# A retention and feed-forward kernel on one core: q scaled after the products instead of before, a new order of work, and other placements

## The chip, the cores and the metric

The kernel runs on one core of a Trainium2 chip. Its engines work at the same time, each through its own list of instructions in order: TensorE (PE; the loads of its weights are PEld), VectorE (DVE), ScalarE (ACT), GpSimd (POOL) and SyncE (SP). Here GpSimd and SyncE only issue DMA transfers. The metric is the device time of one execution in microseconds (us), as the median of several.

## The reference

Eight batches of eight heads, 576 positions of 64 values: each head's scores are multiplied by a matrix that falls off with distance and is zero for later positions, without a softmax. The result, 4608 rows of 512, goes through two layers of 2048 and 512 with a leaky ReLU between. All inputs are float32.

```python
scores = scale * np.matmul(q, k.transpose(0, 1, 3, 2))
gamma = 1.0 - 2.0 ** (-5.0 - np.arange(H, dtype=np.float32))
rel = pos[:, None] - pos[None, :]
Dmat = np.where(rel >= 0, gamma[:, None, None] ** rel[None, :, :], 0.0)
attn_out = np.matmul(scores * Dmat[None], v)
x = attn_out.transpose(0, 2, 1, 3).reshape(B * S, H * D)
h = x @ w_in
out = np.maximum(0.01 * h, h) @ w_out
```

## The kernel before

**Tiling.** The 4608 rows are cut into 36 blocks u of 128 rows (two chunks of 64) and nine groups g of 512 rows (four blocks). All heads of a block are handled together.

**Attention of a block.** Three loads (`ld{u}.0`, `.1`, `.2` for q, k, v; line 346) bring float32 tiles `t`. The falling-off factor gamma^(i-j) is split: q is multiplied by gamma^r times the scale, v by gamma^-r, where r is the place of the row in a stretch of 256 rows. `cq`, `ck`, `cv` (lines 371, 375, 381) make 16-bit tiles from them: k is cast, q and v are scaled by a table in the constants `cs`. On VectorE a scaling is one instruction; on ScalarE it is eight, one for each head. q and k are then turned, by TensorE (`tp`, line 411, copied out of PSUM by `yt`, line 418) for the first eight blocks and by a DMA transpose (`tr`, line 397) for the others. `sa` (line 445) makes the scores, `mk` (line 460) masks them, `sb` (line 454) makes the products of k and v, `st` (lines 485 to 491) adds them to a running state, `sx` (lines 503 and 506) casts the state. `ow` and `ca`, or `oa` in the first four blocks (line 542), add the products of scores and v and of q and state in the PSUM tile `ot`. `x` (line 591) copies that out as `xT`, the input of the first layer. `ot` has two halves, and block u+2 uses the half of block u again.

**The two layers.** The first layer of groups 0 and 1 is plain (`h`, line 640, and the leaky ReLU `l`, line 647). From group 2 on (`a{g}.{n}`, line 833) and in the second layer (`b{g}`, line 911), seven products of sums of quarters take the place of eight. The sums are made on VectorE, of the weights once (lines 686 and 715) and of the data for each group (lines 813 and 887). Partial results are copied out of PSUM by `cA`, `u2` and `k5` (lines 772, 783, 786) and added on VectorE (lines 857 and 947).

**What sets the order.** Nothing is scheduled while the kernel is built. `ORDER` is one long list of job names written out by hand or by another program, and each engine gets its jobs in the sequence of that list. `ENGINE` says which of VectorE and ScalarE does a job where either could. `+n@p` is n products of the constant tile `idle` (line 980), whose results nobody reads. The loads of the first twelve blocks and the weights all go through GpSimd's queue, but for q and k of block 0; later q and k go through SyncE's. The weights come in four quarters each (`wi`, line 612, and `wo`, line 621) and are cast on the way. A block's q, k and v buffers are used again four blocks later (`ld=4`).

Of the kernel before, what the change touches and what calls it, by code (L numbers as in the profile page):

```python
# [33 lines left out]
class Plan:  # L34
# [52 lines left out]
    for eng, names in {  # L87
        "DVE": """
            ck0 cq0 sx0.0 yt0.0 cq1 sx0.1 cv1 cq2 sx1.0 yt2.1 ck3 cq3 yt3.1 cv3 sx2.1 yt3.0 cq4 cv4 x3 ck5 cq5
            cv5 yt5.1 cq6 sx5 cv6 cq7 ck7 cv7 yt7.0 b0.cA cv8 ck10 sx8.0 cv9 cq9 cq11 cq12 cv10 b1.cA cv13 ck15  # L90
            cv14 cq14 cv15 cq15 sx13.1 sx14 cq16 cv16 cv17 cq17 cq18 a2.3.k5 sx17.0 cv18 sx18 cq19 a3.1.u2 x17
            cv20 ck21 cq21 sx19 a3.2.k5 cq22 cv22 sx20 ck23 cv23 cq23 x20 cv24 cq25 sx23 a4.2.cA cv25 a4.2.u2
            cq26 cq27 cv27 sx25 a5.0.u2 a5.0.k5 cq28 cq29 cv29 ck30 cq30 cv30 ck31 cv31 cq32 sx30 cq33 ck33
            a6.0.cA cv33 cv34 ck34 cq35 cq34 a6.2.cA b5.u2 cv35 a6.3.u2 x32 a7.0.cA x33 a7.0.k5 b5.21 a7.1.cA
            b6.11 b6.u2 a7.3.cA a7.3.u2 a8.0.k5 b7.k5 a8.2.u2 a8.2.k5 b7.21 a8.3.u2 b8.21
        """,
        "ACT": """
            cv0 yt0.1 x0 ck1 ck2 yt1.1 yt1.0 cv2 yt2.0 x1 sx1.1 sx2.0 x2 sx3.0 ck4 sx3.1 yt4.1 yt4.0 ck6 sx4.1
            x4 yt5.0 x5 yt6.0 yt6.1 sx6 yt7.1 sx7 x7 x6 ck8 b0.11 cq8 ck9 b0.u2 cq10 b0.k5 cv11 ck12 sx9 x8 ck11
            cv12 sx10 cq13 b0.21 x9 ck13 sx11 b1.11 sx12 x10 b1.u2 x11 ck14 a2.0.cA b1.k5 a2.0.u2 a2.0.k5 x12  # L100
            a2.1.cA a2.1.u2 x13 a2.1.k5 ck16 ck17 sx15 a2.2.cA a2.2.u2 b1.21 a2.2.k5 sx16 x14 a2.3.cA x15
            a2.3.u2 ck18 b2.cA a3.0.cA b2.11 a3.0.u2 a3.0.k5 a3.1.cA cv19 b2.u2 x16 a3.1.k5 ck19 b2.k5 a3.2.cA
            ck20 cq20 a3.2.u2 cv21 b2.21 ck22 x18 a3.3.cA a3.3.u2 a3.3.k5 x19 b3.cA a4.0.cA b3.11 sx21 ck24
            a4.0.u2 a4.0.k5 cq24 a4.1.cA a4.1.u2 sx22.1 a4.1.k5 x21 b3.u2 ck25 b3.k5 ck26 sx24 a4.2.k5 x22 cv26
            a4.3.cA x23 a4.3.u2 a4.3.k5 ck27 b3.21 a5.0.cA b4.cA ck28 cv28 sx26.0 b4.11 x24 ck29 a5.1.cA a5.1.u2
            a5.1.k5 x25 sx27 sx28 b4.u2 a5.2.cA x26 sx29 b4.k5 a5.2.u2 a5.2.k5 x27 a5.3.cA ck32 a5.3.u2 cv32
            a5.3.k5 cq31 b4.21 x28 x29 sx31.1 a6.0.u2 a6.0.k5 sx32 b5.cA a6.1.cA b5.11 a6.1.u2 x30 a6.1.k5 x31
            a6.2.u2 a6.2.k5 sx33 b5.k5 ck35 a6.3.cA a6.3.k5 sx34 sx35.0 a7.0.u2 b6.cA a7.1.u2 a7.1.k5 a7.2.cA
            a7.2.u2 b6.k5 a7.2.k5 x34 x35 a7.3.k5 a8.0.cA b6.21 a8.0.u2 b7.cA b7.11 a8.1.cA b7.u2 a8.1.k5
            a8.1.u2 a8.2.cA a8.3.cA a8.3.k5 b8.cA b8.u2 b8.k5 b8.11x so8.11x b8.11y  # L110
# [941 lines left out]
```

## Time and profile before

| | us |
|---|---|
| median of three runs | 279.86 |
| lowest and highest of the three | 279.4, 282.3 |
| the profiled execution, its time | 279.54 |
| the profiled execution, its span | 277.7 |

The span runs from the first to the last instruction; the time has 1.8 us more around it. The granted clock of TensorE was 0.999 over the span. In the rows further down an engine's busy time is the union of its instructions' spans, and TensorE's ends are modelled: a matmul of 256 columns is shown with 273 ns, while eight of them in a row take 0.87 us. A row of the stages begins with the stretch and its length, and ends with the clock, the share of time in which the DMA engines were busy, and GB/s.

How fast DMA moved things (mean busy share of the 16 DMA engines, in 40 slices) and what each kind of load took from its issue to its landing (us, median):

```profile
DMA  7999999997899999799999998799041100300123
...
t<-in_q_dram POOLq DMA_DIRECT2D x10, 256.0 KB, 8.5
t<-in_k_dram POOLq DMA_DIRECT2D x10, 256.0 KB, 6.5
w_in<-in_moe_w_in_dram POOLq DMA_DIRECT2D x4, 512.0 KB, 7.8
w_out<-in_moe_w_out_dram POOLq DMA_DIRECT2D x4, 512.0 KB, 9.7
```

### The profile page before, as it was taken

What the parts mean: (1) busy time and instruction counts of PE and PEld (TensorE: products, weight loads), DVE (VectorE), ACT (ScalarE), POOL (GpSimd) and SP (SyncE); (2) the same over time, 40 slices, a digit from 0 to 9 for tenths busy, and PEclk for the clock granted to TensorE, in tenths of its full rate; (3) what the DMA queues carried; (4) which work ended last, traced back from release to release, by engine and by line L of the source; (5) the groups of instructions that cost most, each with busy time, mean ns of one, the idle gap of its engine ahead of it and who ended that gap; (6) DMA issues with size and microseconds to landing.
All of it is one profiled execution on the core that took longest, in us unless ns stands there. A gap on an engine that the chain in (4) does not pass through costs nothing.

```text
span 277.7 us, 10117 instructions
## 1 busy us (share of the span) xinstructions
PE 268.1 (97%) x4337; PEld 224.4 (81%) x4337; DVE 229.8 (83%) x431; ACT 206.7 (74%) x459; POOL 72.4 (26%) x92
## 2 busy tenths in 40 slices
PE   6878999999999999999999999999999999999994
PEld 2545688888888888888888888888888888888884
DVE  2767767989998999899999999898989885955761
ACT  3846678769977998999889998899765756665630
POOL 8959696401211313222113321120011000200200
PEclk9999999999999999999999999999999999999999
DMA  7999999997899999799999998799041100300123
GB/s 219 224 240 238 293 287 269 277 216 177 208 256 220 220 295 227 173 236 230 257 222 255 183 228 183 170 247 219 20 139 74 44 2 2 153 0 0 78 97 132
DMA packets 94364, 50.04 MB, mean 180 GB/s; under 512 B 83312, under 2 KB 88560, under 8 KB 94320
## 3 DMA queue, kind: packets, MB, share of 16 engines
q1 hardware_dynamic: 82624, 21.37, 40.4%
q0 software_dynamic: 11264, 27.79, 36.1%
q8 instruction: 34, 0.56, 0.8%
q10 hardware_dynamic: 432, 0.24, 0.3%
q14 instruction: 10, 0.08, 0.1%
HBM read 36.81 MB, written 9.44 MB: 167 GB/s over the span
## 4 chain that ended last, share of the span: by engine, by line
PE 91%; DMA 5%; POOL 1%; ACT 1%; issue 1%; DVE 1%; POOLq 0%
PE acc L911 39%; PE acc L833 32%; PE acc L640 10%; DMA t<-in_k_dram 5%; PE ot L542 5%; PE sc L454 2%; PE sc L445 2%; PE sc L911 1%; POOL t L346 1%; PE acc L411 1%; DVE s L487 0%; POOL w_in L612 0%; ACT st L503 0%; DVE qk L375 0%; DVE s L460 0%
## 5 line engine op out<-in xcount | busy, mean ns | idle before, releaser
L911 PEld LDWEIGHTS <-gt 128*128 128x128 f16 x720 | 69.8, 98 | 8.4
L346 POOL DMA_DIRECT2D t<-in_v_dram x40 | 34.2, 857 | 100.5 <-DVE v L375 64.0
L911 PE MATMUL acc<-w_out,gt 128*128 128x256 f16 x416 | 51.5, 273 | 0.0
L833 PEld LDWEIGHTS <-w_in 128*128 128x128 f16 x448 | 42.4, 98 | 5.6
L853 ACT ACTIVATE gt<-acc 128x512 f16<-128x512 f32 x56 | 33.4, 599 | 16.6 <-PE acc L833 16.4
L861 ACT ACTIVATE gt<-sum 128x512 f16<-128x512 f32 x56 | 34.8, 633 | 4.7 <-DVE sum L857 4.7
L911 PE MATMUL acc<-w_mix,gt 128*128 128x256 f16 x288 | 36.2, 273 | 0.0
L833 PEld LDWEIGHTS <-w_sum 128*128 128x128 f16 x336 | 32.2, 98 | 4.1
L833 PE MATMUL acc<-xs,w_sum 128*128 128x256 f16 x224 | 33.6, 273 | 0.0
L833 PE MATMUL acc<-xT,w_in 128*128 128x256 f16 x224 | 33.5, 273 | 0.0
L833 PE MATMUL acc<-xs,w_in 128*128 128x256 f16 x224 | 33.4, 273 | 0.0
L730 POOL DMA_DIRECT2D out_dram<-osb x16 | 11.5, 718 | 83.9 <-ACT acc L772 38.5
L640 PE MATMUL acc<-xT,w_in 128*128 128x256 f16 (+2 forms) x272 | 30.8, 266 | 0.7 <-ACT qkT L418 0.4
L911 PEld LDWEIGHTS <-mix 128*128 128x128 f16 x288 | 28.1, 98 | 3.3
L460 DVE TENSOR_TENSOR s<-sc,cs 128x512 f16<-128x512 f32 x36 | 24.6, 684 | 4.4 <-PE sc L445 2.3
L640 PEld LDWEIGHTS <-w_in 128*128 128x128 f16 x272 | 22.0, 98 | 5.8 <-issue 0.9
L857 DVE TENSOR_TENSOR sum<-acc,k 128x512 f32<-128x512 f32 x28 | 19.2, 686 | 7.9 <-PE acc L833 5.7
L647 ACT ACTIVATE gt<-acc 128x512 f16<-128x512 f32 x32 | 18.2, 601 | 6.3 <-PE acc L640 6.2
L786 ACT COPY k<-acc 128x512 f32<-128x512 f32 x29 | 17.0, 588 | 7.5 <-PE acc L833 3.7
L375 DVE TENSOR_TENSOR qk<-t,cs 128x512 f16<-128x512 f32 x30 | 20.5, 684 | 2.3 <-DMA t<-in_q_dram 2.3
L591 ACT CAST xT<-ot 128x512 f16<-128x512 f32 x31 | 18.2, 588 | 4.6 <-PE ot L542 4.6
L381 ACT ACTIVATE v<-t,cs 128x64 f16<-128x64 f32 x72 | 18.3, 343 | 4.1 <-DMA t<-in_v_dram 3.4
(69 smaller groups left out, 469.7 us busy)
## 6 DMA issues: line engine op xcount, KB each, us to landing
t<-in_v_dram POOLq DMA_DIRECT2D x32, 256.0 KB, 5.1
out_dram<-osb POOLq DMA_DIRECT2D x16, 512.0 KB, 4.5
t<-in_k_dram SPq DMA_DIRECT2D x22, 256.0 KB, 4.8
t<-in_q_dram SPq DMA_DIRECT2D x22, 256.0 KB, 5.0
t<-in_q_dram POOLq DMA_DIRECT2D x10, 256.0 KB, 8.5
t<-in_k_dram POOLq DMA_DIRECT2D x10, 256.0 KB, 6.5
w_in<-in_moe_w_in_dram POOLq DMA_DIRECT2D x4, 512.0 KB, 7.8
w_out<-in_moe_w_out_dram POOLq DMA_DIRECT2D x4, 512.0 KB, 9.7
```

The costliest lines, as they stand in the source:

```text
L346: engine[eng].dma_start(out=t[CH * j : CH * j + rows], in_=(q, k, v)[x][b, :, CH * w : CH * w + rows, :].rearrange("h t d -> t h d"),)
L375: engine[e].tensor_tensor(out=view[0](out), in0=view[1](t32[u, 2 * x][:]), in1=view[1](decay(u, x)), op=MUL)
L381: nc.scalar.mul(out=out[:, at(h), :], in_=t32[u, 2 * x][:, h, :], mul=tab_sb[:, w, x, h : h + 1])
L460: landed[u] = nc.vector.tensor_tensor(out=s[:], in0=sc[:, :, 0], in1=mask_sb.unsqueeze(1).unsqueeze(1).to_broadcast([P, 2, NP, CH]), op=MUL,)
L591: moved[u] = copies[xe](out=x_of(u).rearrange("q c (j t) -> q j c t", j=2), in_=at)
L640: nc.tensor.matmul(out=a[:, n, :], lhsT=w_in16[:, c, (f0 + n) * P : (f0 + n + 1) * P], rhs=x[:, c, t0 : t0 + nt], start=(n == 0 and c == 0 ...
L647: nc.scalar.activation(out=y[:, f0 : f0 + nf, t0 : t0 + nt], in_=a[:], func=mybir.ActivationFunctionType.Lrelu)
L833: nc.tensor.matmul(out=r[:, f, :], lhsT=w[:, c, (2 * n + f) * P : (2 * n + f + 1) * P], rhs=rhs[:, c, :], start=fresh and c == 0 and f == ...
L853: w = op(what, "ACT", lambda: nc.scalar.activation(out=to(), in_=r[:], func=lr), after, [y], [r])
L857: what, "DVE", lambda: nc.vector.tensor_tensor(out=s[:], in0=r[:], in1=plus[:], op=ADD),
L861: f"l{g}.{n}.{what}", "ACT", lambda: nc.scalar.activation(out=to(), in_=s[:], func=lr), [j], [y],
L911: nc.tensor.matmul(out=(r[tb] if isinstance(r, tuple) else r)[:, tb, :], lhsT=lhs[n]()[:, f, tb * P : (tb + 1) * P], rhs=rhs[n][:, f, :], ...
```

## The change

The factor of q depends on the row alone, and a row of q becomes a column of `ot` for each head. So `cq` is now a plain cast, and `x`, now always on VectorE, multiplies `ot` by a table `q_tab` while it copies it out. The table has a value for each head, place in the stretch of 256 rows, and row. Four VectorE jobs `tb0` to `tb3` make it at the start from two small factors in `cs`, which grows from 148 to 236 values a partition. The tile `stmp` goes (the state is scaled in place), the float states get a pool of three of their own, `idle` becomes a piece of `w_mix`, and a tile `pad` makes the weights begin at a multiple of 512 bytes. `ENGINE` and `ORDER` are new. In `ORDER`, q goes first on SyncE, and GpSimd issues the loads of blocks 0 to 3 ahead of the first quarter of w_in. There are 38 idle products instead of 33. 24 of the 36 `cq` are now on ScalarE (6 before); 24 `ck` are, as before; 6 `cv` (9 before); 19 `sx` jobs (25 before); 94 of the 111 `cA`, `u2` and `k5` (87 before).

```diff
 CFG = dict(
     ap=4,
+    fp=3,
...
-    ld0.1 ld0.2 ld0.0 ld1.0 ld1.1 ld2.1 ck0 ld2.0 cq0 ld1.2 cv0 cq1 ld2.2 +13@3 tp1.0@0 wi1 tp0.0@1 tp0.1@2 sb0 +4@3
+    tb1 tb0 ld0.0 ld0.2 ld0.1 ld1.1 tb3 ld1.2 cq0 ck0 +9@3 tp0.0@3 tb2 ld1.0 yt0.0 +6@1 tp0.1@0 cv0 ld2.1 yt0.1 ck1
...
-    idle = const_pool.tile([P, TOK], F16, name="idle")
-    warm = const_pool.tile([P, 1], FP, name="warm")
+    q_tab = const_pool.tile([P, NB, NP, CH], FP, name="q_tab")
+    pad = const_pool.tile([P, 48], FP, name="pad")
+    warm = pad[:, 0:1]
+    idle = w_mix[:, 2, 0:2].rearrange("p f n -> p (f n)")
...
+    def q_table():
+        for a in range(NB):
+            def run(a=a):
+                nb = CH // FINE
+                nc.vector.tensor_tensor(
+                    out=q_tab[:, a].rearrange("p c (b r) -> p c b r", b=nb),
+                    in0=fine_sb.unsqueeze(2).to_broadcast([P, NP, nb, FINE]),
+                    in1=coarse_sb[:, :, a].unsqueeze(3).to_broadcast([P, NP, nb, FINE]), op=MUL,
+                )
+            steep.append(add(f"tb{a}", "DVE", run))
...
-        def cq():
-            scaled(t[:, 0], 0, qe, lambda h: 2 * (h % NP) + h // NP, (by_half, in_halves))
+        def plain(x, e):
+            copies[e](out=by_half(t[:, x]), in_=in_halves(t32[u, x][:]))
...
-            moved[u] = copies[xe](out=x_of(u).rearrange("q c (j t) -> q j c t", j=2), in_=at)
+            moved[u] = nc.vector.tensor_tensor(
+                out=x_of(u).rearrange("q c (j t) -> q j c t", j=2), in0=at, in1=by_place, op=MUL
+            )
...
-        copied[u] = add(f"x{u}", xe, cp, [j], [xT[u // 4]], [ot_banks])
+        copied[u] = add(f"x{u}", "DVE", cp, [j] + [steep[p] for p in sorted({p0, p1})], [xT[u // 4]], [ot_banks])
```

GpSimd's list at the start, before and after; `t_0`, `t_1`, `t_2` are tiles of q, k and v, and a block whose chunks lie in two batches takes two loads (x2). Before, the loads of blocks 0 (v), 1 and 2, a quarter of w_in, then blocks 3 and 4:

```order
L346 DMA t_2_137<-in_v_dram 128x8x64
L346 DMA t_0_141<-in_q_dram 128x8x64
L346 DMA t_1_143<-in_k_dram 128x8x64
L346 DMA t_1_145<-in_k_dram 128x8x64
L346 DMA t_0_149<-in_q_dram 128x8x64
L346 DMA t_2_152<-in_v_dram 128x8x64
L346 DMA t_2_165<-in_v_dram 128x8x64
L612 DMA w_in_122<-in_moe_w_in_dram 128x4x512
L346 DMA t_1_220<-in_k_dram 128x8x64
L346 DMA t_0_226<-in_q_dram 128x8x64
L346 DMA t_1_260<-in_k_dram 64x8x64 x2
L346 DMA t_2_293<-in_v_dram 128x8x64
```

and after, from the third of these loads on:

```order
L364 DMA t_2_146<-in_v_dram 128x8x64
L364 DMA t_0_167<-in_q_dram 128x8x64
L364 DMA t_1_185<-in_k_dram 128x8x64
L364 DMA t_0_206<-in_q_dram 128x8x64
L364 DMA t_2_221<-in_v_dram 128x8x64
L364 DMA t_2_223<-in_v_dram 128x8x64
L364 DMA t_1_264<-in_k_dram 128x8x64
L364 DMA t_0_314<-in_q_dram 128x8x64
L642 DMA w_in_124<-in_moe_w_in_dram 128x4x512
L364 DMA t_0_326<-in_q_dram 64x8x64 x2
L642 DMA w_in_124<-in_moe_w_in_dram 128x4x512
L364 DMA t_1_361<-in_k_dram 64x8x64 x2
```

The three loads of block 3 (v, k, q) moved from behind the first quarter of w_in to ahead of it, and the three quarters that follow stand between single loads of block 4.

VectorE's list at the start, before; here `t` and `qk` are a block's tiles, `s_` the float states, `st_` the cast ones:

```order
L371 CAST qk_147<-t_1_135 128x2x4x64
L375 TENSOR_TENSOR qk_147<-t_0_139,cs 128x2x4x64
L375 TENSOR_TENSOR qk_163<-t_0_141,cs 128x2x4x64
L485 COPY s_222<-sc 128x256
L418 COPY qkT<-acc 128x512
L375 TENSOR_TENSOR qk_228<-t_0_149,cs 128x2x4x64
L375 TENSOR_TENSOR v_258<-t_2_152,cs 128x512
```

and after:

```order
L382 TENSOR_TENSOR q_tab<-cs 128x256 x4
L407 TENSOR_TENSOR v_183<-t_2_139,cs 128x512
L403 CAST qk_188<-t_1_143 128x2x4x64
L509 COPY s_208<-sc 128x256
L511 TENSOR_TENSOR s_208<-sc,s_208 128x256
L407 TENSOR_TENSOR v_218<-t_2_146,cs 128x512
```

The scalings of q of blocks 0 to 2 have left this list, the table and v of block 0 have come into it.

VectorE's list where blocks 2 and 3 end, after the change (`ot` times the table into `xT`, among states and masks):

```order
L619 TENSOR_TENSOR xT<-ot,q_tab 128x2x4x64
L511 TENSOR_TENSOR s_485<-sc,s_412 128x256
L484 TENSOR_TENSOR s_487<-sc,cs 128x512
L619 TENSOR_TENSOR xT<-ot,q_tab 128x2x4x64
L484 TENSOR_TENSOR s_554<-sc,cs 128x512
L619 TENSOR_TENSOR xT<-ot,q_tab 128x2x4x64 x2
```

Before, the results of blocks 0 to 2 were copies in ScalarE's list, and block 3's alone was here; now all four are multiplications here, the last two behind the mask of block 3.

More of the change, by code (lines that the diff above doesn't have):

```diff
@@ L100 @@
[L100 to L109, printed above, removed]
@@ new lines @@
+    a3.1.p3.0 sx19 ld22.1 ow17 l3.0.12 sx18 ca18 sb20 a3.1.11 a3.1.p7.0 a3.2.p1.0@0 a3.1.12 b2.p4.0 cv21 a3.1.22
+    l3.1.12 st20.0 b2.p4.1 a3.2.cA@1 ck22 x17 a3.1.p4.0 ld25.2 a3.2.p2.0 l3.1.22 b2.21 a3.3.p1.0@2 mk18 st20.1 tr20
+    m3.0.0 m3.1.0 a3.1.21 so2.0 ld23.0 ld24.0 a3.2.11 sb21 ow18 a3.3.cA@3 ca19 cv22 a3.2.p6.0 a3.2.p5.0@0 x18
+    a3.3.p6.0 mk19 cq22 a3.3.p2.0 sx20 a3.2.u2 a3.2.p7.0 a3.2.k5 a3.2.p3.0 ow19 st21.0 cq24 ca20 a3.3.11 a3.2.22
+    a3.3.u2 a3.3.p5.0@2 a3.3.p7.0 ld26.2 a3.2.p4.0 x19 a3.3.k5 a3.2.12 tr21 a3.3.p3.0 b3.p1.0@0 a3.3.22 a3.3.12
@@ new lines @@
+    xs6.3 a6.1.p5.0@3 m5.1.0 a6.0.p4.0 cv32 b5.11 ld35.0 a6.1.p1.0@1 st31.1 ow29 cv34 m5.1.1 sb32 ca30 b5.p6.0 mk30
+    a6.0.21 a6.1.cA@0 a6.1.k5 a6.1.p6.0 a6.1.p3.0 a6.1.u2 a6.1.p2.0 x29 a6.1.11 l6.0.22 a6.1.p7.0 a6.1.22 tr33 ow30
+    ca31 a6.2.p1.0@1 a6.1.p4.0 b5.p6.1 a6.1.21 a6.1.12 st32.0 l6.1.12 b5.p5.0@3 st32.1 sx31.1 a6.2.cA@0 a6.2.p2.0
+    sx32 b5.u2 a6.2.11 cv33 tr34 mk31 a6.2.p6.0 b5.p5.1 x30 a6.2.p5.0@1 a6.2.u2 sb33 b5.k5 a6.2.k5 m5.3.1 ow31 ca32
+    m5.3.0 l6.1.22 st33.0s ld35.1 st33.1 a6.2.p7.0 a6.2.22 a6.2.p3.0 a6.2.12 x31 b5.p3.0 b5.p3.1 a6.2.p4.0
@@ L248 @@
     kinds = sorted({(place(2 * n), place(2 * n + 1)) for n in range(NU)})
-    tab = np.zeros((P, len(kinds), 2, H))
+    tab = np.zeros((P, len(kinds), H))
     for w, at in enumerate(kinds):
         r = np.concatenate([CH * a + np.arange(CH) for a in at])[:, None] - BLK / 2
-        tab[:, w, 0] = gamma[None, :] ** r * scale
-        tab[:, w, 1] = gamma[None, :] ** (-r)
+        tab[:, w] = gamma[None, :] ** (-r)
+    NB, FINE = BLK // CH, 16
+    fine, coarse = np.zeros((P, NP, FINE)), np.zeros((P, NP, BLK // FINE))
+    for c in range(NP):
+        for oo in range(2):
+            rows = slice(CH * oo, CH * oo + CH)
+            fine[rows, c] = gamma[2 * c + oo] ** np.arange(FINE)
+            coarse[rows, c] = gamma[2 * c + oo] ** (FINE * np.arange(BLK // FINE) - BLK / 2) * scale
     s_idx = np.arange(P) % CH
@@ L368, in casts, with cv @@
         ke, qe, ve = by(f"ck{u}", "ACT"), by(f"cq{u}", "DVE"), by(f"cv{u}", "DVE")
-        def ck():
-            copies[ke](out=by_half(t[:, 1]), in_=in_halves(t32[u, 1][:]))
-        def scaled(out, x, e, at, view):
-            if e != "ACT":
-                engine[e].tensor_tensor(
-                    out=view[0](out), in0=view[1](t32[u, 2 * x][:]), in1=view[1](decay(u, x)), op=MUL
-                )
+        def plain(x, e):
+            copies[e](out=by_half(t[:, x]), in_=in_halves(t32[u, x][:]))
+        def cv():
+            if ve != "ACT":
+                engine[ve].tensor_tensor(out=s[:], in0=t32[u, 2][:], in1=decay(u), op=MUL)
                 return
@@ L488, in st @@
                 else:
-                    tmp = t_pool.tile([P, NP, CH], FP, name="stmp")
-                    nc.vector.tensor_tensor(out=tmp, in0=x, in1=before[0][:, before[1]], op=ADD)
+                    nc.vector.tensor_tensor(out=to, in0=x, in1=before[0][:, before[1]], op=ADD)
                     nc.vector.tensor_tensor(
-                        out=to, in0=tmp, in1=gblk_sb.unsqueeze(2).to_broadcast([P, NP, CH]), op=MUL
+                        out=to, in0=to, in1=gblk_sb.unsqueeze(2).to_broadcast([P, NP, CH]), op=MUL
                     )
```

241 lines of the change are left out of this document (125 added, 116 removed), and 12 rows, old and new, of the table loads.

## The prediction

> **What bounds the kernel now.** I read the page first, then the chain of waits in its first 30 us, then the busy time by stage, then the waits of TensorE, and last the timeline of the start. The page's busy row and its by-engine line of the chain:
>
> ```profile
> PE 268.1 (97%) x4337; PEld 224.4 (81%) x4337; DVE 229.8 (83%) x431; ACT 206.7 (74%) x459; POOL 72.4 (26%) x92
> PE 91%; DMA 5%; POOL 1%; ACT 1%; issue 1%; DVE 1%; POOLq 0%
> ```
>
> TensorE is nearly the whole path. The only other thing of size on it is DMA, 5% of 277.7 us. The chain in order of time says where that is (start, length, what):
>
> ```profile
> 3.18 4.42 DMA t<-in_k_dram
> ...
> 7.63 0.68 POOL w_in L612
> 8.31 8.90 DMA t<-in_k_dram
> ...
> 22.60 1.05 PE acc L640 x16
> ...
> 25.30 2.75 PE acc L640 x12
> 28.05 0.22 PE acc L411 x4
> ```
>
> Two loads of k make up the 13.3 us. The second is k of the fourth block (block 3): it stood in GpSimd's queue behind the first quarter of w_in and landed at 17.2 us. From 25 us on the path is TensorE alone. The stages (TensorE, weight loads, VectorE, ScalarE, GpSimd; busy us and instructions):
>
> ```profile
> 0.00:28.00 28.00, 22.11 (x371) 12.49 (x372) 16.82 (x37) 16.02 (x39) 22.88 (x32) 1.00 0.96 230
> 42.00:98.00 56.00, 55.86 (x1032) 47.94 (x1030) 51.37 (x97) 45.88 (x110) 15.31 (x19) 1.00 1.05 231
> 98.00:168.00 70.00, 70.00 (x1242) 60.56 (x1239) 67.79 (x132) 65.87 (x155) 15.29 (x19) 1.00 1.07 230
> 168.00:196.00 28.00, 28.00 (x508) 24.07 (x506) 25.73 (x50) 23.61 (x55) 3.22 (x4) 1.00 0.89 191
> PEld L542 <- issue: 4.6, 21, 0.4
> PEld L454 <- issue: 1.7, 8, 0.2
> ```
>
> After 28 us TensorE has no idle time that counts. The last two rows are the waits of its weight loads between 28 and 270 us: 29 short ones, 0.2 us each, where a run of small attention products is entered. So the change can gain in the first 28 us, a little at those entries, and nothing else; past 28 us it can mostly lose.
>
> **The change part by part.** Prices (group, busy us, mean ns of one):
>
> ```profile
> L375 DVE TENSOR_TENSOR qk<-t,cs 128x512 f16<-128x512 f32 x30 | 20.5, 684 | 2.3 <-DMA t<-in_q_dram 2.3
> L381 ACT ACTIVATE qk<-t,cs 128x64 f16<-128x64 f32 x48 | 12.2, 345 | 0.0
> L371 DVE CAST qk<-t 128x512 f16<-128x512 f32 x12 | 5.5, 466 | 5.0 <-DMA t<-in_k_dram 5.0
> L371 ACT CAST qk<-t 128x512 f16<-128x512 f32 x24 | 14.8, 622 | 2.3 <-DMA t<-in_k_dram 2.3
> L591 ACT CAST xT<-ot 128x512 f16<-128x512 f32 x31 | 18.2, 588 | 4.6 <-PE ot L542 4.6
> L591 DVE CAST xT<-ot 128x512 f16<-128x512 f32 x5 | 3.4, 685 | 0.5 <-PE ot L542 0.5
> L460 DVE TENSOR_TENSOR s<-sc,cs 128x512 f16<-128x512 f32 x36 | 24.6, 684 | 4.4 <-PE sc L445 2.3
> L487 DVE TENSOR_TENSOR s<-sc,s 128x256 f32<-128x256 f32 x40 | 16.7, 418 | 3.0 <-PE sc L454 2.3 <-PE sc L445 0.5
> ```
>
> *q only cast.* VectorE scaled 30 q tiles, 20.5 us; it now casts 12 at 0.466, 5.6 us. ScalarE scaled 6 (48 pieces), 12.2 us; it now casts 24 at 0.622, 14.9 us. *Decay multiplied into the result.* All 36 copies from `ot` become VectorE multiplications of a PSUM tile by an SBUF table. That is the form of L460, 0.684, so VectorE gains 31 of them, 21.2 us, and ScalarE loses 18.2 us. *The table* is four products of 128x256, bounded by L487: 1.7 us, in the first 6 us, while VectorE waits for v of block 0 anyway; without that cover it would put the start 1.7 us later. Other operations that the new order hands from engine to engine, counted in its lists: VectorE takes 3 more scalings of v (+2.1), 6 more state casts (at most +2.5) and 7 fewer PSUM copies (-4.8); ScalarE 3 fewer v (three times 8 pieces), 6 fewer casts, 7 more copies, about -5.7. Sum: VectorE -20.5+5.6+21.2+1.7+2.1+2.5-4.8 = +7.8 us; ScalarE about -21 us.
>
> Does VectorE's work stay covered? Past the table it is 6.1 us more over 36 blocks, 0.17 a block. From 98 to 168 us twelve results are copied, so 67.8 becomes 69.9 of 70 us, which looks full. But spans overlap: in the timeline below two of 0.69 start 0.60 apart. Each instruction then holds the engine some 0.08 less than its span, 132 of them 10 us, and 70 us have about 60 us of work. TensorE's instructions cover it, and I cost it at nothing; the second rival takes that cover away.
>
> *Loads.* "Multiples of 512 bytes" moves little. Adding up the tiles, the q, k and v buffers began at 75776 = 148 x 512 already, and begin at 79360 = 155 x 512 now; what moves onto a multiple are the weight tiles, which lay 480 bytes past one. I take 0, with no trace of it either way; between them and the first product there will be slack (below), so up to 2 us earlier or later would not show.
>
> *Order of the start.* This is the main term. The timeline of the start:
>
> ```profile
> 1.23 4.35 PE L980 MATMUL acc<-idle 128*128 128x512 f16 x13 [1.23 <-DVE idle L316]
> 6.10 2.02 ACT L381 ACTIVATE v<-t,cs 128x64 f16<-128x64 f32 x8 [2.97 <-DMA t<-in_v_dram]
> 6.86 0.69 DVE L375 TENSOR_TENSOR qk<-t,cs 128x512 f16<-128x512 f32 x1 [0.71 <-DMA t<-in_q_dram]
> 9.43 0.69 DVE L375 TENSOR_TENSOR qk<-t,cs 128x512 f16<-128x512 f32 x1
> 10.03 0.69 DVE L375 TENSOR_TENSOR v<-t,cs 128x512 f16<-128x512 f32 x1
> 11.56 2.03 ACT L381 ACTIVATE v<-t,cs 128x64 f16<-128x64 f32 x8 [0.47 <-DMA t<-in_v_dram]
> 13.45 1.69 PE L980 MATMUL acc<-idle 128*128 128x512 f16 x7
> 15.06 0.32 PE L445 MATMUL sc<-qkT 64*64 64x64 f16 x16
> 15.34 0.30 PE L542 MATMUL ot<-s,v 64*64 64x64 f16 x16
> 15.47 0.64 PE L542 MATMUL ot<-qkT,st 64*64 64x64 f16 x16
> 16.80 0.89 POOL L346 DMA_DIRECT2D t<-in_q_dram x1 [3.03 <-DMA w_in<-in_moe_w_in_dram]
> 17.97 0.40 PE L411 MATMUL acc<-ident,qk 128*128 128x128 f16 x4 [1.33 <-DVE qk L371]
> ```
>
> GpSimd's first load (v of block 0) was there at 6.1, its second at 6.85: one load each 0.76 us. The seventh was there at 11.5, where this pace gives 10.65, so up to 0.9 late. In the new order seven, eight, nine and ten are v2, v3, k3, q3: 10.65, 11.4, 12.2, 12.9, or 0.9 later. The first w_in quarter follows. Before, 5.3 us passed between the seventh load (11.5) and the end of a wait for w_in (16.8). So it is there by 18.2, or by 19.1 with late loads. That is k3 five us earlier, which is the ceiling of this term; the floor is nothing.
>
> How much of the five arrives follows by walking the new lists with these spans. ScalarE scales v3 from 11.4 to 13.4, casts k3 to 14.0 and q3 to 14.6. TensorE has by then been through 29 idle products (the first nine cold, 0.33 each by the row of thirteen; the others under 0.24) and the attention of blocks 0 and 1 but for late pieces, turns k3 at 14.65, does v3's states to 15.2, turns q3 to 15.5. ScalarE copies the turned tiles by 16.15, the scores of block 3 stand at 16.55, VectorE masks them at 16.75 to 17.4 (behind the mask of block 2 and the result of block 1). TensorE writes the result of block 3 at 17.5 to 18.3, then five idle products stand in its list, 1.1 us, and the first w_in product starts at 19.3. VectorE multiplies results 3 and 2 by 19.6, as the second product group needs them. Everything that these groups read has landed by then.
>
> Where was before at this point? The groups of the first 28 us:
>
> ```profile
> L411 PE MATMUL acc<-ident,qk 128*128 128x128 f16 x46 | 4.1, 221 | 3.6 <-DVE qk L375 2.2 <-DVE qk L371 1.3
> 0.00:28.00 28.00, 5.82 (x44) 3.56 (x44) 1.00 0.96 230
> ```
>
> The second row is L640 alone: at 28.0 it had done 5.8 us of first-layer products, and 14 transposes past the 32 of blocks 0 to 3, about 0.9 us at 0.23 per four. With the entries the same work takes 6.8 us without a break, so from 19.3 the changed kernel has it at 26.1. Gain 1.9 us, own range 0.4 (late loads, and 0.6 of waits that the walk misses) to 3.4 (a walk that is 1.5 too slow, as it would be without the five idle products and one wait).
>
> *Entries.* From the first w_in product on, the new list enters attention 38 times where the old did 43. Five times 0.2 us is 1.0; since a wait was seen at 29 of 43 entries, I take 0.7.
>
> Sum against the profiled execution, 279.54 us with a span of 277.7: 279.54 - 1.9 - 0.7 = 276.9. The median of the runs shown is 279.86, so this is 1.1% under it. A measurement of this kernel tells about 1% from no change, so "faster" begins below 277.1 and "slower" above 282.7.
>
> **The rivals.** *The start gains nothing.* The loads come in the late way, 0.9 us behind, VectorE and ScalarE meet them in another order than the walk has, and the first w_in product starts near 21.2. For it: before, the seventh load was late. Against it: the walk has 0.5 to 2 us of slack at most steps. Time: 279.54 - 0.7, or up to 0.5 more than before: 279 to 280.
>
> *Slower: the result waits on VectorE.* A block's sum in `ot` is now always emptied by VectorE, in its list's order, behind work that waits for TensorE. Two blocks on, TensorE writes the same half of `ot`, and the products of the next group read xT. If TensorE must stand still for one multiplication, that is 0.685 us a time. Four such stalls give the gain back (2.6 / 0.685), nine and more make it slower by over 1% (5.8 / 0.685): with one at each third block, 11 of 32, it is 276.9 + 7.5 = 284.4. For it: the 69.9 of 70 above. Against it: the real load of 60 of 70, and the 21 us taken from ScalarE, which can release other waits earlier.
>
> *Faster: the rest closes up too.* TensorE's weight loads are busy 24.1 of 28 us in the middle. If a new order could bring that to what the last full stage reaches, the middle would shrink.
>
> ```profile
> 252.00:274.00 22.00, 22.00 (x203) 19.61 (x201) 14.26 (x22) 9.09 (x18) 1.43 (x2) 1.00 0.21 79
> ```
>
> That is 89% against 86%, so 3% of the 168 us from 28 to 196, 5 us: 276.9 - 5 = 272. Against it: the small attention products cause the difference, and they are all still there. The Trainium skill, Perfetto Trace Analysis, section Identifying the Most-Contended Engine, has this as a rule: matmul busy time is no good measure of headroom, and LDWEIGHTS busy is one. By that rule 81% on the page is a TensorE with room, and this rival is the rule's outcome; the rows bear it out only in part, since no wait of over 0.4 us is left there.
>
> **How the numbers follow.** My forecast (275.4 to 278.4) has 0.6, the start without gain 0.18, slower by VectorE 0.1, the rest closing up 0.12. Of the forecast a little over half, 0.36, lies below 277.1; with the last rival 0.48 is faster by over 1%. Slower is the second rival's 0.1. The other 0.42 is within 1%. The range, 273.5 to 280.2, holds the forecast and the start without gain, and the near part of the closing up; it leaves out the slower rival and about 0.08 of the last, just under 2 in 10.
>
> **What would show it.** Right: in the chain no DMA from about 8 us on; k of block 3 cast before 14.6; the first L640-type product between 18.8 and 20 us, TensorE idle before it small; no TensorE wait for VectorE's multiplication after 28 us; the last product near 271 instead of 273.9. Wrong: the first product at 21 or later (the start), or waits of TensorE or its weight loads released by the multiplication into xT (VectorE), or a stage from 28 to 196 us that holds more instructions per us (the rest closing up).

## The result, and the profile after

| | before | after |
|---|---|---|
| median, us (six runs each) | 279.69 | 288.78 |
| lowest and highest | 279.12, 282.3 | 286.77, 289.99 |
| profiled execution: time, span | 279.54, 277.7 | 286.77, 285.0 |

The ratio is 1.030, with an interval of 1.026 to 1.035: slower by 9.1 us, where the forecast was 2.6 us faster. The profiled execution of after is its quickest; the others, at a granted clock of 0.982 against its 0.987, have no trace. So the traces show 7.2 us of the 9.1. For the other 1.9 us the clocks and spans give an estimate: at most (1 - 0.982) x 287.0 - (1 - 0.987) x 285.0 = 1.5 us more of lost clock. The ratios below leave out executions over 1.5% above the quickest of their kernel.

The page of after: busy time, TensorE and its granted clock in 40 slices, and the chain by engine.

```profile
PE 270.9 (95%) x4342; PEld 226.1 (79%) x4342; DVE 236.1 (83%) x450; ACT 188.7 (66%) x381; POOL 72.5 (25%) x92
PE   8999999629999999999999999999999999999995
PEclk9999999968999999999999999999999999999999
PE 91%; DMA 5%; DVE 1%; issue 0%; ACT 0%
```

Each slice is 7.1 us. The loss is in two of them, near 55 us, and the clock is low in two. The chain still has 5% of DMA, but no longer in the loads of k at the start. In order of time:

```profile
18.61 1.19 PE acc L1010 x5
19.79 3.53 PE acc L670 x48
...
47.32 15.31 DMA qkT<-qk
```

The first w_in product (L670) comes at 19.8 and nothing of DMA stands ahead of it. Then one transfer takes 15.3 us: the transpose of block 8, the first that is done by DMA. TensorE's timeline beside it (start, length; idle time and its releaser in brackets):

```profile
53.46 1.04 PE L941 MATMUL acc<-w_out,mix 128*128 128x256 f16 x8
54.42 0.32 PE L478 MATMUL sc<-v,qk 64*64 64x64 f16 x16
62.68 0.31 PE L565 MATMUL ot<-qkT,st 64*64 64x64 f16 x6 [7.93 <-DMA qkT<-qk]
```

The same stretch in before, and then the stages of after (TensorE, weight loads, VectorE, ScalarE, GpSimd, granted clock, DMA share, GB/s):

```profile
54.70:62.70 8.00, 8.00 (x111) 7.00 (x110) 7.00 (x12) 5.71 (x18) 0.00 (x0) 1.00 1.02 225
```

```profile
54.70:62.70 8.00, 0.07 (x11) 0.02 (x4) 2.68 (x4) 0.84 (x4) 0.89 (x1) 0.79 1.09 170
62.70:66.13 3.43, 3.43 (x39) 2.51 (x39) 2.52 (x5) 0.60 (x1) 0.00 (x0) 0.50 1.17 230
66.13:70.00 3.87, 3.87 (x37) 3.47 (x36) 3.80 (x9) 0.84 (x2) 0.00 (x0) 1.00 1.11 172
70.00:84.00 14.00, 14.00 (x286) 12.09 (x285) 10.61 (x20) 7.72 (x20) 3.21 (x4) 1.00 0.92 220
```

TensorE stands 7.9 us, and then works 3.4 us at half its clock, which costs 0.5 x 3.43 = 1.7 us more. (The clock falls to one half at 59.30 us, still in the wait, and is whole again at 66.13; from 62.7 to 70 us its mean is 0.77.) With 2.1 us won at the start (below) that is 7.9 + 1.7 - 2.1 = 7.5, where 7.2 are seen. The same transpose by its issues (tile, queue, count, us from issue to landing), in before, and then in after with the load of k that SyncE issued behind it:

```profile
qkT<-qk SPq DMA_TRANSPOSE x1, 3.6
```

```profile
t<-in_k_dram SPq DMA_DIRECT2D x1, 256.0 KB, 15.2
qkT<-qk SPq DMA_TRANSPOSE x1, 15.3
```

Before, SyncE issued it at 56.36 us, with the last quarter of w_out landed at 55.91. The new order casts q8 early, so it was issued at 47.32, with a w_out quarter and more in GpSimd's queue. That quarter landed at 57.41. What all queues moved from 52 to 57 us in after, in 40 slices of 0.125 us:

```profile
DMA  9997369969999999999990020016990939651929
GB/s 320 158 231 35 66 104 248 227 143 207 412 365 195 283 225 285 223 145 174 137 109 0 0 37 0 0 35 84 424 348 0 412 78 485 125 10 35 406 59 449
```

From 54.6 to 55.5 us hardly a packet began on the DMA engines, though both queues had work.

### The profile page after: what moved, and what is told of

It reads as the page before. It is cut to its first block, busy times and chain, and to the rows that moved or that the text cites. A ratio compares the mean times of both kernels' runs of the same rounds, so it can differ in the third digit from the quotient of the medians.

```text
span 285.0 us, 10053 instructions
## 1 busy us (share of the span) xinstructions
PE 270.9 (95%) x4342; PEld 226.1 (79%) x4342; DVE 236.1 (83%) x450; ACT 188.7 (66%) x381; POOL 72.5 (25%) x92
## 4 chain that ended last, share of the span: by engine, by line
PE 91%; DMA 5%; DVE 1%; issue 0%; ACT 0%
PE acc L941 37%; PE acc L863 31%; PE acc L670 9%; DMA qkT<-qk 5%; PE ot L565 5%; PE acc L1010 3%; PE sc L478 2%; PE sc L469 2%; PE sc L941 1%; PE acc L435 1%; DVE s L484 0%; DVE s L511 0%; DVE s L514 0%; DVE s L509 0%; ACT osb L975 0%
## 5 line engine op out<-in xcount | busy, mean ns | idle before, releaser
L941 PE MATMUL acc<-w_out,gt 128*128 128x256 f16 x416 | 52.1, 273 | 0.0
L863 PEld LDWEIGHTS <-w_in 128*128 128x128 f16 x448 | 42.7, 98 | 5.7 <-DVE sum L887 0.2
L883 ACT ACTIVATE gt<-acc 128x512 f16<-128x512 f32 x56 | 33.3, 601 | 12.8 <-PE acc L863 12.2
L891 ACT ACTIVATE gt<-sum 128x512 f16<-128x512 f32 x56 | 33.9, 630 | 7.7 <-DVE sum L887 7.7
L941 PE MATMUL acc<-w_mix,gt 128*128 128x256 f16 x288 | 36.3, 273 | 0.0
L863 PEld LDWEIGHTS <-w_sum 128*128 128x128 f16 x336 | 31.8, 98 | 4.7 <-issue 0.6
L863 PE MATMUL acc<-xs,w_sum 128*128 128x256 f16 x224 | 33.9, 273 | 0.3 <-issue 0.3
L863 PE MATMUL acc<-xT,w_in 128*128 128x256 f16 x224 | 33.3, 273 | 0.0
L863 PE MATMUL acc<-xs,w_in 128*128 128x256 f16 x224 | 33.0, 273 | 0.0
L403 ACT CAST qk<-t 128x512 f16<-128x512 f32 x48 | 29.3, 623 | 5.5 <-DMA t<-in_q_dram 3.7
L670 PE MATMUL acc<-xT,w_in 128*128 128x256 f16 (+2 forms) x272 | 31.3, 271 | 0.0
L813 ACT COPY u<-acc 128x512 f32<-128x512 f32 x35 | 20.6, 588 | 10.6 <-PE acc L941 5.8
L619 DVE TENSOR_TENSOR xT<-ot,q_tab 128x512 f16<-128x512 f32 x36 | 24.3, 683 | 3.2 <-PE ot L565 3.2
L670 PEld LDWEIGHTS <-w_in 128*128 128x128 f16 x272 | 22.5, 99 | 5.3 <-issue 0.2
L975 ACT COPY osb<-acc 128x512 f32<-128x512 f32 (+1 forms) x15 | 8.4, 558 | 21.5 <-PE acc L941 21.4
L802 ACT COPY acc<-acc 128x512 f32<-128x512 f32 x30 | 17.2, 572 | 8.0 <-PE acc L863 3.4
```

Source lines behind the costliest of these rows:

```text
L403: copies[e](out=by_half(t[:, x]), in_=in_halves(t32[u, x][:]))
L619: moved[u] = nc.vector.tensor_tensor(out=x_of(u).rearrange("q c (j t) -> q j c t", j=2), in0=at, in1=by_place, op=MUL)
L670: nc.tensor.matmul(out=a[:, n, :], lhsT=w_in16[:, c, (f0 + n) * P : (f0 + n + 1) * P], rhs=x[:, c, t0 : t0 + nt], start=(n == 0 and c == 0 ...
L802: copies[ce](out=B[:], in_=A[:])
L813: op("u2", ue, lambda: copies[ue](out=u2[:], in_=B[:]), [done["6"]], [u2], [B])
L863: nc.tensor.matmul(out=r[:, f, :], lhsT=w[:, c, (2 * n + f) * P : (2 * n + f + 1) * P], rhs=rhs[:, c, :], start=fresh and c == 0 and f == ...
```

## The experiments

Theory 1: the transpose shares the DMA engines with GpSimd's full queue, is slow there, and TensorE waits for it. Theory 2: the loss is the new order or VectorE's multiplication, and only surfaces at that wait. Ratios are to the kernel before, run beside them.

| kernel | median, us | ratio, interval |
|---|---|---|
| turn8_by_tensor | 280.64 | 1.003 [1.000, 1.006] |
| late_use8 | 286.06 | 1.023 [1.018, 1.028] |
| late_turn8 | 283.24 | 1.012 [1.004, 1.019] |
| decay_only | 286.73 | 1.024 [1.018, 1.029] |
| late_turn8_ck12 | 280.69 | 1.002 [0.997, 1.006] |
| early_turn8 | 283.03 | 1.009 [1.005, 1.014] |
| off512 | 300.84 | 1.065 [1.057, 1.073] |
| loads_only | 279.49 | 0.997 [0.994, 1.000] |
| off_weights | 281.73 | 1.007 [1.003, 1.011] |
| plain_copy | 287.21 | 1.024 [1.017, 1.031] |
| start_order | 285.35 | 1.019 [1.013, 1.025] |
| k12_early | 281.40 | 1.006 [1.002, 1.010] |
| k12_early_k15_late | 280.36 | 1.001 [0.997, 1.005] |

**Block 8 turned by TensorE** (turn8_by_tensor), in `ORDER` and `CFG`:

```diff
-    turned=8,
+    turned=9,
...
-    h1.10.256@2 h1.14.256@1 tr8 l1.10.256
+    h1.10.256@2 h1.14.256@1 tp8.1@0 yt8.1 tp8.0@0 yt8.0 l1.10.256
```

> The changed kernel with block 8 turned by TensorE (products with the identity, copied by ScalarE) and no longer by a DMA transpose; nothing else moved. Theory 1, the loss is the wait for the transpose that shares the DMA engines with GpSimd's full queue: the 7.93 us stand before L565 at 54.7 us goes, and with it the low granted clock of 62.7 to 70 us (0.77, some 1.7 us); 16 products at 6.1 us for 64 of them come in their place in two groups of 8 (0.8 us at most). 286.8 - 7.9 - 1.7 + 0.8 = 278, so 277 to 279, ratio to before 0.99 to 1.0; the last quarter of w_out lands by 55 us rather than at 57.41. Theory 2, the loss is in the new order as a whole (VectorE's multiplications among it), and the transpose only shows where it surfaces: block 9 or the waits for w_out take its place, and the time stays above 284.

Measured: 280.64, 8.1 us less than the changed kernel. The 7.9 us are gone, and the clock is 1.0. Block 9's transpose, now the first, went out at 49.78 and met the same queue:

```profile
qkT<-qk SPq DMA_TRANSPOSE x1, 13.8
```

Its use stands far enough behind. So one transpose and what hangs on it made nearly the whole loss, and Theory 2 falls as its cause. The time is still 1 us or more above what Theory 1 gave. The trace has two waits of 0.7 us for ScalarE's copies of the turned block at 54 us, and two at 97 us, 0.9 us for another transpose and 0.7 us.

**Its use later, and the transpose later too.** In late_use8 `ca8` goes from behind `b0.cA@3` to just ahead of `mk8`; in late_turn8 also `cq8` goes behind `wm2.1`, and `tr8` behind `wm0.1`.

```diff
-    sx9 b0.p5.0@2 cv11 sb10 m0.3.0 b0.cA@3 ca8 h1.4.256@1 wm2.1 b0.p6.0 wm0.1 b0.p5.1
+    sx9 b0.p5.0@2 cv11 sb10 m0.3.0 b0.cA@3 h1.4.256@1 wm2.1 cq8 b0.p6.0 wm0.1 tr8 b0.p5.1
...
-    m0.3.1 mk8
+    m0.3.1 ca8 mk8
```

> The changed kernel with one word of its order moved: what uses block 8's transpose (ca8) stands after the mixing products that followed it, as in the kernel before. The transpose is issued as early as in the changed kernel. Theory 1: it lands as late as there (61 to 63 us, 13 to 16 us after its issue), since its price is that of the shared DMA engines and not of its use; TensorE works some 6 us past 54.7 us in the meantime, as far as w_out's last quarter (57.41) lets it, so 2 to 4 us of the 7.9 are left: 280 to 283. Theory 2 (the order as a whole): above 285.

> As late_use8, and also block 8's q cast, and so its transpose, behind VectorE's first product with the last quarter of w_out. Theory 1: the transpose is issued at about 55 us, lands 3 to 6 us later, w_out's last quarter lands at 53 to 55 us, no wait of TensorE over 1.5 us between 50 and 65 us: 277 to 279, ratio 0.99 to 1.0. Rival within theory 1, a DMA transpose is slow in this order wherever it stands (a slow first one): it takes over 10 us again, and the time stays above 282.

Measured: the transposes did as Theory 1 has it, 15.8 us early and 4.8 us late (late_use8, then late_turn8):

```profile
qkT<-qk SPq DMA_TRANSPOSE x1, 15.8
```

```profile
qkT<-qk SPq DMA_TRANSPOSE x1, 4.8
```

Both times missed the expectation, 286 and 283, for a reason neither theory named. VectorE's and TensorE's timelines in late_turn8:

```profile
61.22 0.43 DVE L403 CAST qk<-t 128x512 f16<-128x512 f32 x1 [3.21 <-DMA t<-in_k_dram]
```

```profile
64.17 0.32 PE L469 MATMUL sc<-qkT 64*64 64x64 f16 x16 [2.70 <-DVE s L513]
```

The load of k12 follows the transpose on SyncE's queue. VectorE's cast of it stands ahead of block 10's state, for which TensorE waits. In late_use8 that cast waited 4.28 us, and TensorE 3.85 us for the state behind it; w_out's last quarter, at 58.75, cost TensorE 2.26 us more. There the early transpose made what stood beside and behind it late too.

**That cast later** (late_turn8_ck12: `ck12` behind `mk8`):

```diff
-    st10.0 ck12 b0.p6.1
+    st10.0 b0.p6.1
...
-    ca8 mk8 b0.k5
+    ca8 mk8 ck12 b0.k5
```

> late_turn8 with one more word moved: VectorE's cast of k12, at which it stood 3.21 us for a load (with block 10's state and mask queued behind it, and TensorE 2.7 us behind those), stands after them. Theory 1 (the changed kernel's loss is the early transpose in GpSimd's full queue, and what is late behind it): the 2.7 us go, the multiplication and the rest cost nothing, and the gain of the start is left: 276.5 to 279, ratio to before 0.99 to 1.0. Theory 2 (part of the loss is VectorE's multiplication or the new order past 70 us): TensorE's standing is spread over the later stretches, and the time stays above 281.

Measured: 280.69, above the 276.5 to 279 of Theory 1 and not to be told from before. The traced execution took 279.11, so its trace shows the better case. The 2.7 us went. Its stages from 28 to 112 us, its waits of TensorE from 42 to 240 us, and then the stages of before:

```profile
28.00:70.00 42.00, 42.00 (x729) 35.34 (x728) 38.74 (x74) 30.26 (x67) 22.44 (x27) 1.00 1.05 246
70.00:112.00 42.00, 40.37 (x794) 34.46 (x794) 38.94 (x78) 34.71 (x79) 8.18 (x10) 1.00 1.10 249
```

```profile
PE sc L478 <- issue: 1.3, 1, 1.3
PE acc L863 <- DVE sum L887: 0.4, 1, 0.4
```

```profile
28.00:70.00 42.00, 41.86 (x728) 34.62 (x726) 34.64 (x66) 32.10 (x79) 20.06 (x24) 1.00 1.06 253
70.00:112.00 42.00, 42.00 (x777) 36.11 (x775) 40.45 (x80) 36.42 (x80) 8.78 (x12) 1.00 1.07 239
```

Up to 70 us it keeps its lead. From 70 to 112 us TensorE is idle for 1.63 us, in the two waits shown (83 and 95 us), where before has none. The longer one falls inside a run of sixteen like products, after the second. So even without the slow transpose the start's gain is mostly given back.

**The early transpose in the kernel before** (early_turn8). `cq8` goes to VectorE behind `wm2.0`, and `tr8` right behind it:

```diff
-    ld11.1 x6 mk7 l1.14.0 wm2.0 ow7
+    ld11.1 x6 mk7 l1.14.0 wm2.0 cq8 tr8 ow7
```

> The kernel before with block 8's q cast moved from ScalarE to VectorE's place after its first product with w_out at 48.6 us, and the transpose right behind it; its use stays where it was (62 us). Theory 1: issued at 49 to 51 us instead of 56.36, the transpose takes 10 to 14 us instead of 3.59, since w_out's last quarter and five loads are still in GpSimd's queue, and that quarter lands 1 to 4 us later than 55.91; the use of the transpose stands late, so the time grows by 0 to 3 us only: 279.5 to 283. Rival (what made the transpose slow is something of the changed kernel: its alignment, its loads, the k and q loads behind it on SP's queue): it lands 3 to 5 us after its issue, and the time is that of before within 1 us.

Measured: 283.03, slower by 0.5 to 1.4%. Issued at 50.05, it took

```profile
t<-in_k_dram SPq DMA_DIRECT2D x1, 256.0 KB, 14.1
t<-in_q_dram SPq DMA_DIRECT2D x1, 256.0 KB, 14.4
qkT<-qk SPq DMA_TRANSPOSE x1, 14.3
```

and landed at 64.31, where the late one lands at 59.95. TensorE waited 1.9 us for it even at its late use, and had half its clock for 3.4 us from then on. Nothing else of the change is needed for the slow transpose.

**A plain load in its place** (k12_early): late_turn8_ck12 with SyncE's load of k12 where the changed kernel issued the transpose.

```diff
-    h1.14.256@1 l1.10.256
+    h1.14.256@1 ld12.1 l1.10.256
...
-    m0.1.1 ld12.1 st10.0
+    m0.1.1 st10.0
```

> late_turn8_ck12 with the load of k12 on SP's queue issued at 44 to 48 us, where the changed kernel issued its transpose, while GpSimd's queue is still full; the transpose of block 8 stays at 55.8 us. If the full queue slows whatever SP issues beside it: k12's 256 KB land 8 us or more after their issue (k12 took 15.2 us behind the transpose in the changed kernel). If it is the transpose, with its packets of 256 bytes, that fares badly beside GpSimd's queue and slows it in turn: k12 lands 2 to 4 us after its issue, w_out's last quarter at 54.5 to 55.5 us, the transpose 4 to 5 us after its own. The time in both cases that of late_turn8_ck12 within 1 us (279.7 to 281.7).

Measured: issued at 42.40 us, k12 landed after

```profile
t<-in_k_dram SPq DMA_DIRECT2D x1, 256.0 KB, 13.2
```

So the full queue slows whatever SyncE sends beside it: the first branch held, and it needs no transpose. The trace's packets (queue 0 is GpSimd's, 1 SyncE's; count and mean ns of one, in 1.5 us from the time given, without packets of 4 bytes):

```
k12_early    43.0  q0 1024 B x260, 102;  4096 B x17, 169;   no q1
             47.5  q0 1024 B x223, 97;                      q1 256 B x227, 32
             49.0  q0 1024 B x169, 96;   4096 B x35, 166;   q1 256 B x216, 29
             52.0  q0 1024 B x239, 96;                      q1 256 B x197, 31
             61.0  no q0                                    q1 256 B x1608, 18
early_turn8  54.5  q0 1024 B x33, 104;   4096 B x70, 275;   q1 256 B x131, 34
             59.0  q0 4096 B x11, 580;                      q1 256 B x246, 124
             62.0  q0 4096 B x5, 227;                       q1 256 B x201, 101
```

Once its packets start, some 3.5 us after the issue, the load sends one of 256 bytes for about each one of GpSimd's, a seventh of the rate that SyncE's queue had alone, at 61 us. 256 KB are 1024 of them, 64 for each of 16 engines: at 97 + 32 ns a pair that is an estimate of 8.3 us, and nearly all were sent between 46 and 53.5 us. The Trainium skill, DMA: Bandwidth & Descriptors, section Queues, rings and completion order, says that each DMA engine goes round its queues packet by packet; these counts agree. The transpose is a different matter in part: its packets came no faster at 62 us, when GpSimd's queue sent only 5 of its own (its last load landed at 65.55), and GpSimd's packets of 4096 bytes took 275 and 580 ns beside it, 166 beside the plain load. Sharing by turns does not explain that. w_out's last quarter landed at 54.59 beside neither (late_turn8_ck12), at 55.99 beside the plain load, and at 57.41 beside the transpose (the changed kernel).

**One wait more mended** (k12_early_k15_late: the casts `ck15` and `ck14` behind `xs2.2`).

```diff
-    a2.0.11 ck15 cv14 ck14 xs2.3 mk12 xs2.2
+    a2.0.11 cv14 xs2.3 mk12 xs2.2 ck15 ck14
```

> k12_early with VectorE's casts of k15 and k14, at which a load held it before 83 us, some jobs later. If the waits that are left past 70 us are single places of the order that can be mended like this one: the 0.5 us before L863 at 83 us go, 0.5 us less than k12_early, 278.5 to 280.5. If the order's places shift against the loads in each execution, other waits of the same size stand elsewhere, and the time is that of k12_early.

Measured: 280.36. In its trace the wait before L863 at 85 us is 0.2 us, where k12_early has 0.8. But one of 0.5 us has come at 138 us, and that for w_out at 58 us is 1.4 us instead of 1.0; the one before L478 at 97 us is 1.1 instead of 1.4. In all they are 3.2 us in both. So the place was mended and the sum stayed, as the second branch has it; the two medians are 1 us apart with overlapping intervals.

**The start alone** (loads_only: the kernel before, with the loads of k3 and q3 ahead of the first w_in quarter).

```diff
-    wi1 tp0.0@1 tp0.1@2 sb0 +4@3 yt0.1 ld3.1 st0.0 ck1 yt0.0 ld3.0 cq2
+    ld3.1 ld3.0 wi1 tp0.0@1 tp0.1@2 sb0 +4@3 yt0.1 st0.0 ck1 yt0.0 cq2
```

> The kernel before with one part of the change: block 3's k and q loads stand ahead of the first quarter of w_in in GpSimd's queue. By the forecast's sum for the start: q3 and k3 land at 12 to 13.5 us instead of 17.21 and 18.46, w_in's quarter at 17.5 to 18.5 instead of 16.25, the first product with it starts no later than before, and TensorE is 0.5 to 1.9 us ahead at 28 us: 277.6 to 279.2, ratio 0.992 to 0.998. Rival (the start gains nothing, since the order behind it closes the gap at the next load): 279.4 to 280.

Measured: 279.49 against 279.98. k3 landed at 11.71, q3 at 13.05, the quarter at 17.59; L640 had done 6.1 us at 28 us instead of 5.8. Its ratio lies in the range of the first expectation and its time in that of the second, so 0.5 us is no more than a hint of a gain.

**The start's order before the old rest** (start_order: `ORDER` up to `ca4` from the changed kernel, then the words of before that are left; casts and turns of these blocks on the changed kernel's engines).

```diff
-    ld0.1 ld0.2 ld0.0 ld1.0 ld1.1 ld2.1 ck0 ld2.0 cq0 ld1.2 cv0 cq1 ld2.2 +13@3
+    ld0.0 ld0.2 ld0.1 ld1.1 ld1.2 cq0 ck0 +9@3 tp0.0@3 ld1.0 yt0.0 +6@1 tp0.1@0
...
```

> The kernel before, arithmetic and layout unchanged, with the first part of its order (to block 4's first use, some 28 us) taken from the changed kernel and the rest in its own order. If the start's gain of some 2 us at 28 us can be kept where nothing behind it is moved: 277.3 to 278.8, ratio 0.991 to 0.996. If what lies behind gives it back (loads and transposes that come no earlier): 279.3 to 280.5.

Measured: 285.35. TensorE waited for VectorE's masks and states in the start itself:

```profile
PE sc L460 <- DVE s L475: 1.7, 2, 1.4
PE ot L557 <- DVE s L475: 0.8, 1, 0.8
```

Behind such waits the clock was at one half twice, for 3.4 us from 15.8 and from 36.3 us. With scaled q, VectorE did not do that order in time. The question it was to answer stays open.

**The arithmetic alone** (decay_only: the changed kernel with `ORDER` and `ENGINE` of before, `tb0` to `tb3` in front).

```diff
-    tb1 tb0 ld0.0 ld0.2 ld0.1 ld1.1 tb3 ld1.2 cq0 ck0 +9@3 tp0.0@3 tb2
+    tb1 tb0 tb3 tb2 ld0.1 ld0.2 ld0.0 ld1.0 ld1.1 ld2.1 ck0 ld2.0 cq0
...
```

> The changed kernel's arithmetic (q only cast, decay multiplied into the result on VectorE, and its table of decays) and its layout of SBUF, in the order and on the engines of the kernel before. Theory 1: VectorE's 6 us more and ScalarE's 18 us less lie beside TensorE's work, so the time is that of before within 1 us: 279 to 281, ratio 1.00 to 1.005. Rival: the multiplication holds up what TensorE waits for (36 blocks at up to 0.69 us, or every third of them): 282 to 300.

Measured: 286.73, in the rival's range. The page's busy row and chain:

```profile
PE 272.6 (95%) x4337; PEld 226.3 (79%) x4337; DVE 240.6 (84%) x466; ACT 184.2 (64%) x386; POOL 73.5 (26%) x92
PE 67%; DVE 23%; DMA 5%; issue 3%; POOL 0%; ACT 0%; DVEq 0%; POOLq 0%
```

VectorE, with 10.8 us more than before, makes 23% of the path. Of TensorE's waits the multiplication itself ended 1.5 us:

```profile
PE acc L671 <- DVE xT L620: 1.0, 3, 0.3
...
PE ot L566 <- DVE xT L620: 0.5, 2, 0.3
```

After 28 us some 2 us more are waits for VectorE's masks, sums and states; the clock was at one half from 8.2 to 11.7 us. How much of the rest comes from what stands behind the multiplication in VectorE's list is not shown. The changed kernel's own order hands casts and copies to ScalarE, and its waits have nothing of this.

**No multiplication** (plain_copy: late_turn8_ck12 with the result copied on ScalarE, the decay left out).

```diff
-            moved[u] = nc.vector.tensor_tensor(
-                out=x_of(u).rearrange("q c (j t) -> q j c t", j=2), in0=at, in1=by_place, op=MUL
-            )
+            moved[u] = nc.scalar.copy(out=x_of(u).rearrange("q c (j t) -> q j c t", j=2), in_=at)
```

> late_turn8_ck12 with the result copied by ScalarE without the decay (the multiplication with q's decay is left out, 36 products of 0.68 us on VectorE fewer, 36 copies of some 0.59 us on ScalarE more). If what the repaired kernel gives back past 70 us (waits of 0.5 and 1.4 us) is VectorE's load: those go and the time falls to 277 to 278. If VectorE's load is hidden, as the forecast had it, and the waits are those of loads and of the order's timing: within 1 us of late_turn8_ck12 (279.7 to 281.7).

Measured: 287.21, outside both. The 36 copies lengthen ScalarE's list, which was ordered without them; TensorE lost 1.7 us before an L478 at 38 us and 3.5 us in eight smaller waits from 69 us on, seven of them for ScalarE; its clock was at one half from 38.5 to 41.9 us. It does not tell what VectorE's load costs.

**Alignment.** off512 makes the padding 32 bytes longer; off_weights shifts the weights alone:

```diff
-    pad = const_pool.tile([P, 48], FP, name="pad")
+    pad = const_pool.tile([P, 56], FP, name="pad")
```

```diff
-    pad = const_pool.tile([P, 48], FP, name="pad")
+    pad = const_pool.tile([P, 40], FP, name="pad")
...
+    const_pool.tile([P, 8], FP, name="pad_behind")
```

> late_turn8_ck12 with the padding 32 bytes longer, so that all weights, loads and buffers behind it lie 32 bytes past a multiple of 512 bytes in SBUF. By the forecast the alignment is worth nothing: the time of late_turn8_ck12 within 1 us, DMA loads and transposes of the same length. Rival (the alignment is a gain that the collision hid): loads of 256 KB take longer than 0.76 us each in GpSimd's queue, and the time is 2 us or more above late_turn8_ck12.

> late_turn8_ck12 with only the weight tiles 480 bytes past a multiple of 512, where the kernel before had them; the loads of q, k and v and their casts stay at multiples. By the forecast (alignment worth nothing here): the time of late_turn8_ck12 within 1 us, a quarter of w_out still 2.45 us in GpSimd's queue. Rival (the weights' place is part of the gain, as the loads' place proved to be in off512): quarters of 3 us or more and a time 1 us or more above late_turn8_ck12.

Measured: 300.84 and 281.73. The two quickest times of off512 were 297.97 and 298.44, and its trace is of one of 303.23. Loads issued from 28 to 33 us, in off512 and then in late_turn8_ck12:

```profile
t<-in_k_dram POOLq DMA_DIRECT2D x2, 256.0 KB, 9.7
t<-in_v_dram POOLq DMA_DIRECT2D x2, 256.0 KB, 9.6
```

```profile
t<-in_v_dram POOLq DMA_DIRECT2D x3, 256.0 KB, 6.0
t<-in_k_dram POOLq DMA_DIRECT2D x2, 256.0 KB, 5.9
```

In off512 five loads in a row landed 1.2 us apart, where late_turn8_ck12 has 0.76. VectorE's and ScalarE's busy times are those of late_turn8_ck12 (235.9 and 189.1 us against 235.6 and 189.1), so it is the transfers: 32 bytes past a multiple cost a load 0.4 us, and the kernel some 18 us by the two quickest times. What each kind of transfer has of these is not shown. For the weights alone w_out's first two quarters landed at 40.82 and 45.14 us, against 41.22 and 45.34; the median is 1 us higher with overlapping intervals, which settles nothing finer.

No version beats the kernel before by more than can be told: the best is loads_only.

## Why the prediction was wrong

- **The start** was right. Forecast: k3 at 12.2 to 12.9, w_in by 18.2 to 19.1, first product at 19.3. Seen: 12.83, 18.76, 19.63; q3 at 14.44 was 0.6 later than its later bound. Up to 28 us L670 alone had

```profile
0.00:28.00 28.00, 8.25 (x68) 5.32 (x68) 1.00 1.00 242
```

  against 5.82, with 40 transpose products against 46 (0.3 us): 2.1 us ahead, forecast 1.9.
- **The entries** were wrong in sign. Fewer entries did not bring fewer waits: between 28 and 270 us the weight loads of after have

```profile
PEld L565 <- issue: 13.3, 25, 8.0
PEld L478 <- issue: 2.3, 10, 0.4
```

  34 short waits with 7.6 us when the one of 8.0 is taken out, against 29 with 6.3. Instead of -0.7 stands up to +1.3; since the sum above has no room for it, most of that cost nothing.
- **VectorE and ScalarE**: +6.3 and -18.0 us, forecast +7.8 and -21. In the new order this is covered, as forecast: VectorE's multiplication is in no wait of TensorE. decay_only shows that the cover is the work of the new order and placements: the same arithmetic with the old ones costs 7 us, of which the second rival's own mechanism, TensorE held by a multiplication, ends 1.5 us of waits.
- **The failed step** is "past 28 us it can mostly lose", with only entries and VectorE costed there. Of the moved steps I costed the loads of the start and none of the 28 transposes. The new lists showed block 8's cast of q ahead of where it stood, hence SyncE's first transpose 9 us earlier, against a GpSimd queue that I had written down as backed up (6.5 to 9.7 us from issue to landing). That the queue delays another queue's transfer was priced nowhere. It measured 15.3 us instead of 3.6, a wait of 7.9 us and 1.7 us of low clock.
- **That the rest stays as it was** failed too, in smaller measure: with the transpose late, 1.6 us of the start's gain goes again between 70 and 112 us. Single waits of 0.4 to 1.5 us move about from version to version, and for the 1.3 us at L478 the profile names no releaser. What sets them stays open.
- **Alignment at 0** is borne out to about 1 us (off_weights), and only because the loads lay on multiples before; how much hung on it I did not see.
- **The rivals**: slower had 0.1, for another cause. A transfer that meets a full queue was not among them. The rows of before could have raised the question, with 3.6 us for the transpose behind the last quarter and 9.7 us for the quarters, but not the price.

## What to carry to other kernels

When an order is rebuilt, list every transfer whose issue moves and what is in the other queues at its new time; a transpose issued 6 to 9 us earlier, into a full queue, landed 3 to 5 us later than in before, and delayed the loads it met. Put the use of such a transfer where its slow case is covered, or do the work on another engine until the queue is empty. A lead won at the start was mostly lost again here at later waits that did not move with it, and an order that fitted one arithmetic cost 7 us with another. So look through the later waits again after each such change.

## What was not expected of the hardware

- SyncE's queue beside GpSimd's full one sends about one small packet for each of GpSimd's: a load of 256 KB took 13.2 us instead of 3.0.
- A transpose issued there took 13.8 to 15.8 us in four kernels instead of 3.6 to 4.8, little more than the plain load, but it slowed GpSimd's queue as well. Hardly a packet began for 0.9 us in the changed kernel and 1.4 us in late_use8, GpSimd's packets of 4096 bytes took a mean of 543 ns (the changed kernel, 1.5 us from 53.5 us) instead of the 166 beside the plain load, and its own took 101 ns when GpSimd's queue sent hardly any. Why is open.
- Loads of 256 KB into tiles 32 bytes past a multiple of 512 bytes: 1.2 us each in the queue instead of 0.76.
- 4.6 us into a wait of 7.9 us TensorE's granted clock fell to one half, and stayed there for 6.8 us, 3.4 us of them work. It also fell to one half for 3.4 us at waits of 1.7 us (plain_copy), 1.9 us (early_turn8) and 3.9 us (late_use8), but not at one of 2.7 us (late_turn8).
